# A gradient's forward D transform by even and odd d, with D in even/odd order in all tables

## The chip, the cores and the metric

The kernel runs on one core of one Trainium2 chip (trn2). The metric is the device time of one execution in microseconds. A profile's own span (first to last instruction) is some 1.8 us shorter than the time of the same execution. Ratios are the mean time of one kernel's runs over that of the other's runs of the same rounds on the same chip, with a 95% interval, so they are not quite the ratio of the medians that stand beside them. Times of the kernel before differ from chip to chip (medians of 1465.8 to 1468.0 us), so a kernel is compared with the kernel before of its own rounds.

## The reference

The forward function mixes a spectral filter and a gated feed-forward layer; the kernel returns its output and seven gradients.

```python
def _A_ref(x, w_r, w_i):                    # x: 1 x 2048 x 576
    X = rfft2(x.astype(float32), axes=(-2, -1)) * (w_r + 1j * w_i)
    return irfft2(X, s=(S, D), axes=(-2, -1)).astype(bfloat16)
def _B_ref(x, w_gate, w_up, w_down):        # D = 576, F = 4608
    return (_gelu(x @ w_gate) * (x @ w_up)) @ w_down
g = _sigmoid((x * gate_w).sum(-1, keepdims=True))
return g * a + (1 - g) * b                  # ... and its vjp for grad_out
```

The gradient with respect to the filter needs the forward transform of g * grad_out, as well as that of x. This is the transform that the change touches.

## The kernel before

The 2D transform is done by matmuls in steps. Step u1 takes one tile of 128 positions t (of 16), contracts D = 576 in five chunks with a table of cosines (c = 0) and sines (c = 1), and gives l = 0 to 288 (DF = 289) of each. Step u2 does the first part of the transform along S.

```python
def u1(t):
    def f():
        yps = ps()
        for c in range(2):
            for ci in range(5):
                nc.tensor.matmul(yps[:, c, :DF], lhsT=src[:, ci, t, :], rhs=tb.Dt[ci][:, c, :],
                                 start=(ci == 0), stop=(ci == 4))
        ys[t] = unit([2, DF], name="Y")
        # ... x: a plain copy; gradient:
        nc.scalar.activation(ys[t][:], yps[:, :, :DF], ACT.Copy, scale=scale[:, t:t + 1])
    return f
```

The gradient's units are not run by themselves. They are slots between the matmuls of the feed-forward part, which goes over 18 groups g of features, four iterations m in each: z and xy on PE, elementwise steps on DVE and ACT, and from g = 1 on the weight gradients of the group before, again on PE. In group 0 each iteration takes four slots; these are u1 of t = 0 to 8 and u2 of t = 0 to 6. The other seven u1 come later. After them come a middle part (filter products), then the inverse transforms, in the same slots.

Each group's weights are loaded one group ahead, in three parts after the first three iterations. The SP queue issues these loads and most stores of this stage, in order (POOL issues those of the weight gradients):

```python
if part < 2:
    w, cols = (B_w_gate, B_w_up)[part], slice(part * FG, (part + 1) * FG)
    LD.dma_start(wgu[:, 0:4, cols], w[0:512, fsl].rearrange("(c p) f -> p c f", p=P))
    for r in (LO, HI):
        LD.dma_start(wgu[r, 4, cols], w[512:D, fsl])
else:
    LD.dma_start_transpose(wdT[:, 4:5, :], B_w_down[fsl, DCH[4][0]:D])
    LD.dma_start_transpose(wdT[:, 0:4, :], B_w_down[fsl, 0:512])
    LD.dma_start(wdT[LO, 4, :], wdT[HI, 4, :])
```

In the middle part, ACT copies a result from PSUM to a tile Vt, which takes one of 19 rotating "unit" buffers, and SP stores it to DRAM (scr_p).

Of the kernel before, what the change touches and what calls it, by code (L numbers as in the profile page):

```python
# [9 lines left out]
ACT = mybir.ActivationFunctionType  # L10
ALU = mybir.AluOpType
BF16 = mybir.dt.bfloat16
# [27 lines left out]
LO, HI = slice(0, 64), slice(64, 128)  # L40
L2 = DF - P
L2NEW = 256 - L2


class Unit:
# [13 lines left out]
def iotas(nc, res, unit):  # L59
    tb = Tables()  # L60
    G = nc.gpsimd
    kw = dict(allow_small_or_imprecise_dtypes=True)
    tb.lrow = unit([DF], F32, name="lrow")
    G.iota(tb.lrow[:], pattern=[[1, DF]], base=0, channel_multiplier=0, **kw)
    tb.dcol = res.tile([P, 5], F32, name="dcol")
    G.iota(tb.dcol[:, 0:4], pattern=[[128, 4]], base=0, channel_multiplier=1, **kw)
    G.iota(tb.dcol[:, 4:5], pattern=[[0, 1]], base=512, channel_multiplier=1, **kw)
    tb.krow = res.tile([P, P], F32, name="krow")
    G.iota(tb.krow[:], pattern=[[1, P]], base=0, channel_multiplier=0, **kw)
    tb.scol = res.tile([P, T], F32, name="scol")  # L70
    G.iota(tb.scol[:], pattern=[[1, T]], base=0, channel_multiplier=16, **kw)
    tb.mrow_i = res.tile([P, P], I32, name="mrow_i")
    G.iota(tb.mrow_i[:], pattern=[[1, P]], base=0, channel_multiplier=0)
    tb.qcol_i = res.tile([P, 1], I32, name="qcol_i")
    G.iota(tb.qcol_i[:], pattern=[[0, 1]], base=0, channel_multiplier=1)
    tb.halfpi = res.tile([P, 1], F32, name="halfpi")
    nc.vector.memset(tb.halfpi[:], math.pi / 2)
    tb.pi = res.tile([P, 1], F32, name="pi")
    nc.vector.memset(tb.pi[:], math.pi * EPS_SCALE)
    tb.npi = res.tile([P, 1], F32, name="npi")  # L80
    nc.vector.memset(tb.npi[:], -math.pi * EPS_SCALE)
    tb.warm = res.tile([P, 1], F32, name="warm")
    nc.scalar.activation(tb.warm[:], tb.halfpi[:], ACT.Sin)
    tb.late = []
    return tb
# [7 lines left out]
def build_D(nc, tb, unit, res):  # L93

    V = nc.vector
    tb.Dt = []
    dn = res.tile([P, 5], F32, name="dn")
    V.tensor_scalar(dn[:], tb.dcol[:], 1.0 / D, None, op0=ALU.mult)
    step = 2.0 * math.pi / D
    for c0 in range(0, 5, 2):  # L100
        n = min(2, 5 - c0)
        TS = (nc.gpsimd if c0 == 4 else V).tensor_scalar
        X = unit([n, DF], F32, name="XD")
        y = unit([n, DF], F32, name="yD")
        for c in range(n):
            TS(y[:, c, :], tb.lrow[:], dn[:, c0 + c:c0 + c + 1], MAGIC, op0=ALU.mult, op1=ALU.add)
        TS(y[:], y[:], -MAGIC, -float(D), op0=ALU.add, op1=ALU.mult)
        for c in range(n):
            V.scalar_tensor_tensor(X[:, c, :], tb.lrow[:], tb.dcol[:, c0 + c:c0 + c + 1], y[:, c, :],
                                   op0=ALU.mult, op1=ALU.add)  # L110
        o = unit([n, 2, DF], name="Dt")
        V.scalar_tensor_tensor(y[:], X[:], -1.0, X[:], op0=ALU.mult, op1=ALU.max)

        r = LO if c0 == 4 else slice(0, P)
        if c0 == 4:
            nc.gpsimd.memset(o[HI, :, :, :], 0.0)

        def sines(o=o, X=X, y=y, r=r):
            nc.scalar.activation(o[r, :, 0, :], y[r], ACT.Sin, bias=tb.halfpi[r], scale=-step)
            nc.scalar.activation(o[r, :, 1, :], X[r], ACT.Sin, scale=-step * EPS_SCALE)  # L120
        tb.late.append(sines)
        tb.Dt += [o[:, c] for c in range(n)]


def build_R(nc, tb, unit, t0):
# [48 lines left out]
def kernel(  # L174
# [34 lines left out]
    dB = wstack.enter_context(tc.tile_pool(name="pdB", bufs=1)).tile([P, T, D], BF16, name="dB")  # L209

    wts = {}

    def load_w(g, part):

        fsl = slice(g * FG, (g + 1) * FG)
        if part == 0:
            wgu = wpool.tile([P, 5, 2 * FG], BF16, tag="wgu", name="wgu")
            wdT = wpool.tile([P, 5, FG], BF16, tag="wdT", name="wdT")
            wts[g] = wgu, wdT
        wgu, wdT = wts[g]  # L220
        if part < 2:
            w, cols = (B_w_gate, B_w_up)[part], slice(part * FG, (part + 1) * FG)
            LD.dma_start(wgu[:, 0:4, cols], w[0:512, fsl].rearrange("(c p) f -> p c f", p=P))
            for r in (LO, HI):
                LD.dma_start(wgu[r, 4, cols], w[512:D, fsl])
        else:
            LD.dma_start_transpose(wdT[:, 4:5, :], B_w_down[fsl, DCH[4][0]:D])
            LD.dma_start_transpose(wdT[:, 0:4, :], B_w_down[fsl, 0:512])
            LD.dma_start(wdT[LO, 4, :], wdT[HI, 4, :])

    nc.gpsimd.memset(gwT[LO, 4:5], 0.0)
    ident = res.tile([P, P], BF16, name="ident")
    make_identity(nc, ident[:])
    tb = iotas(nc, res, unit)
    with nc.allow_non_contiguous_dma(reason="tiny gate_w column load"):
        nc.gpsimd.dma_start(gwT[:, 0:4], gate_w[0:512].rearrange("(c p) -> p c", p=P))
        nc.gpsimd.dma_start(gwT[HI, 4:5], gate_w[512:D].rearrange("(p o) -> p o", o=1))

    def load_x(t0):
# [39 lines left out]
    def tchunk(src, dst, t0):  # L279
        for k, cs in enumerate(((0, 1), (2, 3), (4,))):  # L280
            pool, tag = headps()
            tp_ = pool.tile([P, 2, 2, 4, P], BF16, tag=tag, name="tp")
            for j, c in enumerate(cs):
                for tt in range(4):
                    if c < 4:
                        nc.tensor.transpose(tp_[:, 0, j, tt, :], src[:, t0 + tt, c * P:(c + 1) * P], ident[:])
                    else:
                        for r in (LO, HI):
                            nc.tensor.transpose(tp_[r, 0, 0, tt, :], src[:, t0 + tt, 512:D], ident[:])
            o = dst[:, cs[0]:cs[0] + len(cs), t0:t0 + 4, :]  # L290
            i = tp_[:, 0, 0:len(cs)]
            if k == (t0 // 4) % 2:
                nc.scalar.copy(o, i)
            else:
                V.tensor_copy(o, i)
# [189 lines left out]
    def fwd_units(src, dst, scale, ps=pftile, vevac=None):  # L485
# [16 lines left out]
        def u2(t):  # L502
# [12 lines left out]
                    nc.scalar.copy(Vt[:], vps[:, :, :DF])  # L515
                LD.dma_start(dst[t], Vt[:])
            return f
        return [u1(t) for t in range(T)], [u2(t) for t in range(T)]

    def tail_table():  # L520

        nc.gpsimd.memset(tb.At2[:], 0.0)
        LD.dma_start(tb.At2[L2NEW:P, :, :], tb.Dt[2][0:DF - 256, :, :])

    def zipped(u1, u2):
        out = [u1[0]]
# [129 lines left out]
    def inv_units(s, dv, scale):  # L656
        vp, zt = {}, {}

        def pre(i0):
            def f():  # L660
                vp[i0] = load_V(s, i0)
            f.noslot = True
            return f

        def z(i):
            def f():
                Vp = vp[i // 2 * 2]
                ii = i % 2
                zps = pftile()
                zf = zps[:].rearrange("p a b -> p (a b)")  # L670
                for lc, l0 in enumerate((0, P, L2)):
                    o = zf[:, lc * 256:(lc + 1) * 256]
                    for v in range(2):
                        nc.tensor.matmul(o, lhsT=Vp[:, ii, v, l0:l0 + P],  # L674
                                         rhs=tb.B[:, 1 - v:3 - v, :].rearrange("q v m -> q (v m)"), start=(v == 0), stop=(v == 1))
                zt[i] = unit([6, P], name="ZT")
                nc.scalar.copy(zt[i][:].rearrange("p a m -> p (a m)"), zf[:, 0:768])
            return f

        def d(i):  # L680
            def f():
                Z = zt.pop(i)
                yps = pftile()
                for c in range(2):
                    for lc in range(3):
                        nc.tensor.matmul(yps[:, c, :DF], lhsT=Z[:, 2 * lc + c, :],  # L686
                                         rhs=tb.Dt[lc][:, c, :] if lc < 2 else tb.At2[:, c, :],
                                         start=(lc == 0), stop=(lc == 2))
                ev = unit([2, DF], F32, name="ev")
                yo = unit([D], name="yo")  # L690
                nc.scalar.activation(ev[:], yps[:, :, :DF], ACT.Copy, scale=scale)
                V.tensor_tensor(yo[:, 0:DF], ev[:, 0, :], ev[:, 1, :], op=ALU.add)
                V.tensor_tensor(yo[:, D - 1:DF - 1:-1], ev[:, 0, 1:DF - 1], ev[:, 1, 1:DF - 1], op=ALU.subtract)
                LD.dma_start(dv[:, i, :], yo[:])
            return f
        out = [z(0)]
        for i in range(1, T):
            out += [z(i), d(i - 1)]
            if i % 2 == 1 and i + 3 < T:
                out.append(pre(i + 3))  # L700
        return out + [d(T - 1)], [pre(0), pre(2)]
# [23 lines left out]
    build_B(nc, tb, unit, res)  # L725
    run_late(tb)
    tail_table()
    x2[T - 1]()
    gate()

# [348 lines left out]
```

## Time and profile before

| | before |
|---|---|
| time, median of 6 (the result's rounds) | 1465.84 us (1463.18 to 1466.31) |
| profiled span | 1462.4 us |
| PE / DVE / ACT / POOL busy | 98% / 58% / 47% / 8% |
| u1 of the gradient | 160 matmuls of 289 columns, 124 ns apart |
| group 0, iteration | 10.25 us |
| bound in group 0 (65 to 105 us) | DVE |
| bound after that | PE |

The shares are averages over stages with different limits.

### The profile page before, as it was taken

How to read it: one execution, taken by the hardware profiler on the slowest of the kernel's cores; microseconds unless marked ns; L12 is line 12 of the kernel's file. 1: busy time of each engine (PE TensorE's matmuls, PEld its weight loads, DVE VectorE, ACT ScalarE, POOL GpSimd, SP SyncE). 2: the span in 40 equal slices, each digit the busy share in tenths (PEclk: the TensorE clock that was granted, in tenths of full speed). 3: DMA queues.
4: the chain of work that ended last, by engine and by line, in shares of the span. 5: the costliest groups of instructions: out<-in, count | busy, mean ns of one | idle time of the engine just before them, and what ended most of it. 6: DMA issues, size and time to landing. Idle time of an engine off the chain costs nothing.

```text
span 1462.4 us, 30015 instructions
## 1 busy us (share of the span) xinstructions
PE 1433.0 (98%) x11723; PEld 1068.6 (73%) x11808; DVE 846.0 (58%) x2258; ACT 690.7 (47%) x1355; POOL 118.3 (8%) x203
## 2 busy tenths in 40 slices
PE   7999999999999999999999999999999999999998
PEld 5766777677777677677677677678877777777776
DVE  7697677888887886776776776773000541211100
ACT  5786666766676666666766766662000000000000
POOL 1001011011011001001000000110000100000000
PEclk9999999999999999999999999999999999999999
DMA  5144344455445435334434544657999997878773
GB/s 190 60 127 123 114 126 120 140 146 150 137 132 148 120 117 142 106 110 134 136 104 119 147 126 113 168 135 169 260 195 197 211 205 160 171 157 166 154 149 72
DMA packets 483963, 210.49 MB, mean 144 GB/s; under 512 B 307883, under 2 KB 473932, under 8 KB 483820
## 3 DMA queue, kind: packets, MB, share of 16 engines
q1 hardware_dynamic: 474220, 188.06, 53.6%
q0 software_dynamic: 7792, 19.49, 4.4%
q8 instruction: 92, 1.51, 0.4%
q10 hardware_dynamic: 1808, 1.02, 0.3%
q14 instruction: 51, 0.42, 0.1%
HBM read 40.89 MB, written 93.82 MB: 92 GB/s over the span
## 4 chain that ended last, share of the span: by engine, by line
PE 92%; DVE 3%; issue 1%; ACT 1%; DMA 0%; DVEq 0%; ACTq 0%
PE acc L929 29%; PE wps L443 17%; PE xy L333 16%; PE wps L426 9%; PE z L321 8%; PE wps L456 2%; PE xy L328 2%; PE pf L686 2%; PE z L324 1%; PE pf L674 1%; PE pf L493 1%; PE fx L493 0%; DVE Vt L513 0%; DMA pin<-scr 0%; PE pf L632 0%
## 5 line engine op out<-in xcount | busy, mean ns | idle before, releaser
L929 PEld LDWEIGHTS <-pin 128*128 128x128 bf16 x3456 | 338.0, 98 | 87.1 <-DMA pin<-scr 1.9
L333 PE MATMUL xy<-wgu,xT 128*128 128x512 bf16 x1067 | 257.7, 380 | 9.6 <-issue 7.6
L443 PEld LDWEIGHTS <-xn 128*128 128x128 bf16 x2304 | 225.4, 98 | 32.4 <-issue 0.2
L333 PEld LDWEIGHTS <-xT 128*128 128x128 bf16 x1152 | 106.8, 98 | 137.3 <-issue 29.9
L346 ACT ACTIVATE da<-z,omg 128x256 bf16<-128x256 f32 x288 | 113.2, 474 | 148.0 <-PE z L324 145.0
L946 ACT COPY bo<-acc 128x288 f32<-128x288 f32 x32 | 12.7, 398 | 309.9 <-PE acc L929 251.8
L426 PE MATMUL wps<-dB,A 128*128 128x288 bf16 x1152 | 154.2, 286 | 0.0
L929 PE MATMUL acc<-wd_all,pin 128*128 128x288 bf16 x1152 | 142.8, 286 | 1.6 <-DMA pin<-scr 1.6
L929 PE MATMUL acc<-wgT,pin 128*128 128x288 bf16 x1152 | 143.6, 286 | 0.0
L929 PE MATMUL acc<-wuT,pin 128*128 128x288 bf16 x1152 | 143.6, 286 | 0.0
L321 PE MATMUL z<-wdT,dOT 128*128 128x256 bf16 x1152 | 137.7, 273 | 1.5 <-ACT Y L499 1.2
L426 PEld LDWEIGHTS <-A 128*128 128x128 bf16 x1152 | 112.7, 98 | 35.7
L443 PE MATMUL wps<-dHg,xn 128*128 128x256 bf16 x1152 | 134.4, 273 | 0.0
L443 PE MATMUL wps<-dHu,xn 128*128 128x256 bf16 x1152 | 131.5, 273 | 0.0
L321 PEld LDWEIGHTS <-dOT 128*128 128x128 bf16 x1152 | 111.2, 98 | 18.8 <-issue 5.6
L1003 DVE SCALAR_TENSOR_TENSOR f32t<-gwf,dlog,b16t 128x576 f32<-128x576 f32 x16 | 13.1, 818 | 187.5 <-DMA b16t<-dxa_scr 187.5
L352 ACT ACTIVATE q<-xy 128x512 bf16<-128x512 f32 x144 | 86.0, 597 | 69.6 <-PE xy L333 66.0
L359 DVE TENSOR_SCALAR s<-q 128x512 bf16<-128x512 bf16 x144 | 42.8, 297 | 94.2 <-ACT q L352 92.6
L376 ACT ACTIVATE om<-s 128x512 bf16<-128x512 bf16 x144 | 91.9, 638 | 8.9 <-DVE s L360 8.7
L377 ACT ACTIVATE s<-s 128x512 bf16<-128x512 bf16 x144 | 90.8, 630 | 4.6
L449 POOL DMA_DIRECT2D out_dram<-dw x67 | 48.7, 727 | 540.2 <-ACT dw L404 277.0
L360 DVE TENSOR_TENSOR s<-xb,s 128x512 bf16<-128x512 bf16 x144 | 61.3, 426 | 49.4 <-ACT xb L357 42.8
(182 smaller groups left out, 1807.3 us busy)
## 6 DMA issues: line engine op xcount, KB each, us to landing
scr<-A SPq DMA_DIRECT2D x144, 128.0 KB, 2.1
scr<-dHg SPq DMA_DIRECT2D x144, 128.0 KB, 2.1
scr<-dHu SPq DMA_DIRECT2D x144, 128.0 KB, 2.0
out_dram<-dw POOLq DMA_DIRECT2D x67, 128.0 KB, 2.6
wd_all<-in_B_w_down_dram SPq DMA_DIRECT2D x3, 1728.0 KB, 13.5
out_dram<-dwd POOLq DMA_DIRECT2D x34, 144.0 KB, 2.3
scr_p<-Vt SPq DMA_DIRECT2D x32, 144.5 KB, 2.2
Vp<-scr_p SPq DMA_DIRECT2D x16, 289.0 KB, 3.0
```

The source lines that it names most:

```text
L321: nc.tensor.matmul(zo(t), lhsT=dOT[:, ci, t, :], rhs=wdT[:, ci, :], start=(t % 4 < 2 and ci == 0), stop=False)
L333: nc.tensor.matmul(xy[k][:, t % 2, :], lhsT=xT[:, ci, t, :], rhs=wgu[:, ci, :], start=False, stop=(ci == 3))
L346: nc.scalar.activation(da[:, tt, :], z[:, tt, k, :], ACT.Copy, scale=omg32[:, t:t + 1])
L352: nc.scalar.activation(q[:], xy[:, :, 0:FG], ACT.Square)
L359: V.tensor_scalar(s[:], q[:], A_GELU, 1.0, op0=ALU.mult, op1=ALU.add)
L360: V.tensor_tensor(s[:], xb[:], s[:], op=ALU.mult)
L376: nc.scalar.activation(om[:], s[:], ACT.Sigmoid, scale=-2.0 * C_GELU)
L377: nc.scalar.activation(s[:], s[:], ACT.Sigmoid, scale=2.0 * C_GELU)
L426: nc.tensor.matmul(wps[:, :288], lhsT=tl(0, t)[:, fch * P:(fch + 1) * P], rhs=dB[:, t, h * 288:(h + 1) * 288], start=(t == 0), stop=(t == ...
L443: nc.tensor.matmul(wps[:, cc, :], lhsT=xn[:, t, (c0 + cc) * P:(c0 + cc + 1) * P], rhs=tl(k, t), start=(t == 0), stop=(t == T - 1))
L449: wst[0].dma_start(ov[:, c0:c0 + TPB, fsl], dw[:])
L929: nc.tensor.matmul(acc[:, :288], lhsT=src[:, r, :], rhs=w_of(r)[:, h * 288:(h + 1) * 288], start=(first and r == 0), stop=(last and r == F ...
```

## The change

With l and 288 - l, cosines and sines differ only in sign by the parity of d. So one sum over even d and one over odd d, for l = 0 to 144 only, give all 289 l: their sum is Y[l], their difference is Y[288 - l] reversed. That needs D on the partitions in even/odd order. Chunks 0 and 1 become the even d, 2 and 3 the odd ones; the last 64 d stay together and get a table masked by parity. Since all transforms share the tables, x, dOT and the weights are put into that order too.

```diff
+def half_units(u1):
+    def u(t):
+        def f():
+            yps = pftile()
+            for par in range(2):
+                for j, (ci, tab) in enumerate(((2 * par, tb.Dt[2 * par]), (2 * par + 1, tb.Dt[2 * par + 1]), (4, tb.half[:, par]))):
+                    nc.tensor.matmul(yps[:, par, :2 * HF].rearrange("p (c l) -> p c l", c=2), lhsT=dOT[:, ci, t, :],
+                                     rhs=tab[:, :, 0:HF], start=(j == 0), stop=(j == 2))
+            ev = unit([2, 2, HF], F32, name="ev")
+            Y = u1[t] = unit([2, DF], name="Y")
+            nc.scalar.activation(ev[:].rearrange("p e c l -> p e (c l)"), yps[:, :, :2 * HF], ACT.Copy, scale=g32[:, t:t + 1])
+            E = nc.gpsimd if t < 7 else V
+            E.tensor_tensor(Y[:, :, 0:HF], ev[:, 0], ev[:, 1], op=ALU.add)
+            for c in range(2):
+                E.tensor_tensor(Y[:, c, DF - 1:HF - 1:-1], ev[:, c, c, 0:HF - 1], ev[:, 1 - c, c, 0:HF - 1], op=ALU.subtract)
 ... (load_w)
-        if part < 2:  (w_gate in part 0, w_up in part 1)
+        if part == 0:  (both)
+            for w, c0 in ((B_w_gate, 0), (B_w_up, FG)):
+                cols = slice(c0, c0 + FG)
+                LD.dma_start(wgu[:, 0:4, cols].rearrange("p (e k) f -> p e k f", e=2),
+                             w[0:512, fsl].rearrange("(k p e) f -> p e k f", e=2, p=P))
+                for r in (LO, HI):
+                    LD.dma_start(wgu[r, 4, cols], w[512:D, fsl])
+        elif part == 1:  (the transposes of w_down, the large one into wtmp)
+        else:            (four copies wtmp -> wdT that sort the rows, and wdT[HI] -> wdT[LO])
 ... (build_D, tchunk, the inverse's z and d)
+            nc.tensor.transpose(tp_[:, 0, j, tt, :], src[:, t0 + tt, eo(c)], ident[:])
+                for lc, ls in enumerate((eo(0), eo(2), slice(L2, DF))):
```

More of the change, by code (lines that the diff above doesn't have):

```diff
@@ L42, with eo @@
 L2NEW = 256 - L2
+HF = 145
+def eo(c):
+    return slice(256 * (c % 2) + c // 2, 256 * (c % 2) + 256, 2)
 class Unit:
@@ L65, in iotas @@
     tb.dcol = res.tile([P, 5], F32, name="dcol")
-    G.iota(tb.dcol[:, 0:4], pattern=[[128, 4]], base=0, channel_multiplier=1, **kw)
+    for k in range(2):
+        G.iota(tb.dcol[:, 2 * k:2 * k + 2], pattern=[[1, 2]], base=256 * k, channel_multiplier=2, **kw)
     G.iota(tb.dcol[:, 4:5], pattern=[[0, 1]], base=512, channel_multiplier=1, **kw)
@@ L122, in build_D @@
         tb.Dt += [o[:, c] for c in range(n)]
+    tb.Dt[1], tb.Dt[2] = tb.Dt[2], tb.Dt[1]
 def build_R(nc, tb, unit, t0):
@@ L211 @@
     wts = {}
+    wtmp = [None]
     def load_w(g, part):
@@ L216, in load_w @@
         if part == 0:
-            wgu = wpool.tile([P, 5, 2 * FG], BF16, tag="wgu", name="wgu")
-            wdT = wpool.tile([P, 5, FG], BF16, tag="wdT", name="wdT")
-            wts[g] = wgu, wdT
-        wgu, wdT = wts[g]
-        if part < 2:
-            w, cols = (B_w_gate, B_w_up)[part], slice(part * FG, (part + 1) * FG)
-            LD.dma_start(wgu[:, 0:4, cols], w[0:512, fsl].rearrange("(c p) f -> p c f", p=P))
-            for r in (LO, HI):
-                LD.dma_start(wgu[r, 4, cols], w[512:D, fsl])
-        else:
-            LD.dma_start_transpose(wdT[:, 4:5, :], B_w_down[fsl, DCH[4][0]:D])
-            LD.dma_start_transpose(wdT[:, 0:4, :], B_w_down[fsl, 0:512])
+            wts[g] = (wpool.tile([P, 5, 2 * FG], BF16, tag="wgu", name="wgu"), wpool.tile([P, 5, FG], BF16, tag="wdT", name="wdT"))
+            wgu = wts[g][0]
+            for w, c0 in ((B_w_gate, 0), (B_w_up, FG)):
[4 more added lines that the diff above has]
+                    LD.dma_start(wgu[r, 4, cols], w[512:D, fsl])
+        elif part == 1:
+            wtmp[0] = wpool.tile([P, 4, FG], BF16, tag="wtmp", name="wtmp", bufs=1)
+            LD.dma_start_transpose(wts[g][1][:, 4:5, :], B_w_down[fsl, DCH[4][0]:D])
+            LD.dma_start_transpose(wtmp[0][:], B_w_down[fsl, 0:512])
+        else:
+            wdT = wts[g][1]
             LD.dma_start(wdT[LO, 4, :], wdT[HI, 4, :])
+            for par in range(2):
+                for h, r in enumerate((LO, HI)):
+                    LD.dma_start(wdT[r, 2 * par:2 * par + 2, :], wtmp[0][par:P:2, h:4:2, :])
     nc.gpsimd.memset(gwT[LO, 4:5], 0.0)
@@ L235 @@
     with nc.allow_non_contiguous_dma(reason="tiny gate_w column load"):
-        nc.gpsimd.dma_start(gwT[:, 0:4], gate_w[0:512].rearrange("(c p) -> p c", p=P))
+        for par in range(2):
+            nc.gpsimd.dma_start(gwT[:, 2 * par:2 * par + 2], gate_w[par:512:2].rearrange("(k p) -> p k", p=P))
         nc.gpsimd.dma_start(gwT[HI, 4:5], gate_w[512:D].rearrange("(p o) -> p o", o=1))
@@ L285, in tchunk @@
                     if c < 4:
-                        nc.tensor.transpose(tp_[:, 0, j, tt, :], src[:, t0 + tt, c * P:(c + 1) * P], ident[:])
+                        nc.tensor.transpose(tp_[:, 0, j, tt, :], src[:, t0 + tt, eo(c)], ident[:])
                     else:
@@ L517, in u2, with half_tails @@
             return f
-        return [u1(t) for t in range(T)], [u2(t) for t in range(T)]
+        return ([u1(t) for t in range(T)] if src is xT else half_units(ys)), [u2(t) for t in range(T)]
     def tail_table():
         nc.gpsimd.memset(tb.At2[:], 0.0)
-        LD.dma_start(tb.At2[L2NEW:P, :, :], tb.Dt[2][0:DF - 256, :, :])
+        for par in range(2):
+            LD.dma_start(tb.At2[L2NEW + par:P:2], tb.Dt[1 + 2 * par][0:17 - par])
+    def half_tails():
+        mi = res.tile([P, 1], I32, name="par_i")
+        V.tensor_single_scalar(mi[:], tb.qcol_i[:], 1, op=ALU.bitwise_and)
+        mask = res.tile([P, 2], F32, name="par_f")
+        V.tensor_copy(mask[:, 1:2], mi[:])
+        V.tensor_scalar(mask[:, 0:1], mask[:, 1:2], -1.0, 1.0, op0=ALU.mult, op1=ALU.add)
+        tb.half = unit([2, 2, HF], name="half")
+        for par in range(2):
+            V.tensor_scalar(tb.half[:, par], tb.Dt[4][:, :, 0:HF], mask[:, par:par + 1], None, op0=ALU.mult)
+    def half_units(u1):
+        def u(t):
+            def f():
+                yps = pftile()
+                for par in range(2):
+                    for j, (ci, tab) in enumerate(((2 * par, tb.Dt[2 * par]), (2 * par + 1, tb.Dt[2 * par + 1]), (4, tb.half[:, par]))):
[8 more added lines that the diff above has]
+                    E.tensor_tensor(Y[:, c, DF - 1:HF - 1:-1], ev[:, c, c, 0:HF - 1], ev[:, 1 - c, c, 0:HF - 1], op=ALU.subtract)
+            return f
+        return [u(t) for t in range(T)]
     def zipped(u1, u2):
@@ L670, in f @@
                 zf = zps[:].rearrange("p a b -> p (a b)")
-                for lc, l0 in enumerate((0, P, L2)):
+                for lc, ls in enumerate((eo(0), eo(2), slice(L2, DF))):
                     o = zf[:, lc * 256:(lc + 1) * 256]
                     for v in range(2):
-                        nc.tensor.matmul(o, lhsT=Vp[:, ii, v, l0:l0 + P],
+                        nc.tensor.matmul(o, lhsT=Vp[:, ii, v, ls],
                                          rhs=tb.B[:, 1 - v:3 - v, :].rearrange("q v m -> q (v m)"), start=(v == 0), stop=(v == 1))
@@ L686, in f @@
                         nc.tensor.matmul(yps[:, c, :DF], lhsT=Z[:, 2 * lc + c, :],
-                                         rhs=tb.Dt[lc][:, c, :] if lc < 2 else tb.At2[:, c, :],
+                                         rhs=tb.Dt[2 * lc][:, c, :] if lc < 2 else tb.At2[:, c, :],
                                          start=(lc == 0), stop=(lc == 2))
@@ L727 @@
     tail_table()
+    half_tails()
     x2[T - 1]()
```

## The prediction

> **What bounds the kernel now.** I read the page first (busy shares, slices, costly groups), then the busy time by stretch, then the chain of work that ended last for the stretch in which the gradient's forward transform starts, and last the timeline there.
>
> ```profile
> PE 1433.0 (98%) x11723; PEld 1068.6 (73%) x11808; DVE 846.0 (58%) x2258; ACT 690.7 (47%) x1355; POOL 118.3 (8%) x203
> L493 PE MATMUL pf<-Dt,dOT 128*128 128x289 bf16 x160 | 22.2, 287 | 1.1 <-DVE Vt L513 1.0
> ```
>
> PE is busy nearly everywhere, and the changed matmuls are the 160 of line 493 on dOT. The mean of 287 ns is the trap here: matmuls overlap, so it is a latency and not what one costs. The cost is the spacing. The chain shows it:
>
> ```profile
> 57.95 2.48 PE pf L493 x20
> 60.42 1.73 PE xy L333 x8
> 62.65 1.25 PE pf L493 x10
> 63.98 0.74 ACT Y L499
> 64.72 0.53 ACT om L376
> 65.27 0.43 DVE om L381
> ...
> 102.21 2.24 DVE dB L774 x8
> 104.45 0.68 DVE Vt L513
> 105.17 1.40 PE pf L493 x10
> 106.57 1.75 PE wps L443 x16
> ```
>
> Twenty matmuls of 289 columns take 2.48 us, so 124 ns each. The second thing to see is more important: from 65.27 to 105.17 us the chain is on DVE (so are all the pieces that I left out at the "..."). Before and after it is on PE. That stretch is the first feature group (g = 0), which has no weight gradients to give PE work. The stretches say the same (columns: window, then busy time of PE, PEld, DVE, ACT, POOL):
>
> ```profile
> 75.02:85.28 10.26, 9.86 (x68) 6.08 (x69) 9.71 (x27) 8.55 (x17) 0.00 (x0) 1.00 0.48 138
> 300.00:600.00 300.00, 297.08 (x2375) 214.51 (x2403) 245.75 (x654) 202.99 (x404) 29.45 (x46) 1.00 0.48 136
> ```
>
> In the first of them, one of the group's four iterations (10.26 us), DVE works 9.71 us with no named wait. PE's 9.86 is inflated by the overlap: by spacing I count 16 z matmuls 1.75, 16 full xy 3.6, half-depth ones 0.7, two D transforms 2.5, two S transforms 1.0, in all about 9.5 us. From 300 to 600 us it is PE that is full and DVE has 18% to spare.
>
> [...]
>
> **Part 1, fewer matmuls.** Per t, 10 matmuls of 289 columns become 6 of 290: 10 x 124 - 6 x 124.5 = 493 ns less PE time. Sixteen units give 7.9 us (0.54%), the ceiling of the change; with the latency of 287 ns it would have looked like 18 us. Where do they lie? Group 0 takes four transform slots in each of four iterations, 16 slots, which are u1 of t = 0 to 8 and u2 of 0 to 6. So nine units lie in group 0 and seven in the PE-bound rest. **Seven units: -3.45 us on the path.** Of the nine, t = 0 and 1 (the x20 piece) lie before DVE takes over; ACT evicts Y twice there and only then copies xb, on which DVE waits:
>
> ```profile
> 61.71 0.43 DVE L360 TENSOR_TENSOR s<-xb,s 128x512 bf16<-128x512 bf16 x1 [2.80 <-ACT xb L357]
> ```
>
> PE is 0.99 us earlier there. But the new half tables put five small DVE operations (three of about 0.16 us by the rows for one column, two of about 0.2 us) in front of omg, for which ACT waits 0.72 us, so ACT is some 0.5 us later and then continuous: omg, four da, q, two Y, xb. I count xb to start at 60.35 instead of 61.10: **-0.75 us**. The other seven of group 0 shorten PE beside a busy DVE: **0**.
>
> **Part 2, the combination.** Y was one ACT eviction (742 ns). Now the eviction goes to f32 (580 columns; the inverse's ev shows that f32 output is no slower) and three additions follow, of 290, 144 and 144 elements, on POOL for t < 7 and on DVE from 7 on. On DVE the like operation is this one:
>
> ```profile
> 700.47 0.47 DVE L692 TENSOR_TENSOR yo<-ev 128x289 bf16<-128x289 f32 x1 [1.66 <-ACT ev L691]
> 700.84 0.45 DVE L693 TENSOR_TENSOR yo<-ev 128x287 bf16<-128x287 f32 x1
> 701.21 0.29 DVE L359 TENSOR_SCALAR s<-q 128x512 bf16<-128x512 bf16 x1
> ```
>
> It costs 0.37 us of spacing; 144 elements about 0.22; so 0.81 us for one Y. For t = 7 and 8, inside DVE's stretch: **+1.6 us**. From t = 9 on it falls on a DVE with slack: 0.
>
> [...] But POOL is not free for DVE. The start of the program shows it:
>
> ```profile
> 3.61 1.20 DVE L109 SCALAR_TENSOR_TENSOR XD<-lrow,dcol,yD 128x289 f32<-128x289 f32 x2
> 7.22 0.95 DVE L109 SCALAR_TENSOR_TENSOR XD<-lrow,dcol,yD 128x289 f32<-128x289 f32 x2
> ```
> ```profile
> 3.90 0.60 POOL L106 TENSOR_SCALAR yD<-lrow,dn 128x289 f32<-128x289 f32 x1
> ```
>
> The same DVE pair takes 0.25 us longer beside one POOL operation of 0.60 us. Line 112 is 0.11 us longer beside POOL's 0.52 us. Together DVE lost a third of POOL's time (0.36 of 1.12). [...] I choose 0.5 per Y, because the author's boundary at t < 7 hints that POOL was found cheaper than DVE's 0.81. Y of t = 0 meets an idle DVE; t = 1 to 6 meet a full one: 6 x 0.5 = **+3.0 us**.
>
> **Part 3, order and tables.** Group weights: 13 transfers instead of 9 per group, one contiguous transpose into a temporary and 256 KB copied inside SBUF; they are issued an iteration or more before use, with DMA under half busy: 0. Strided loads (128 transposes in the head, 128 of Vp in the inverse): 0. Startup: one more iota and gate_w transfer on POOL, about 0.1 us on dn: 0. The store queue starts some 2 us later behind four more copies, with units to spare: 0.
>
> **Sum:** -3.45 - 0.75 + 1.6 + 3.0 = +0.4 us, so 1465.9 us.
>
> **The rivals.** [...] (b) POOL is free for DVE, or DVE's stretch gives way to the shorter PE: ACT waits 0.87 us per iteration for line 493 before Y. Then 1465.55 - 3.45 - 0.75 + 1.6 = 1463, and 1458 if all 7.9 us come through. Against: the chain does not touch PE there. (c) Weight loads with a step of two are slow. If they took 196 ns instead of 98, the 128 loads of Vp would space their matmuls by 196 instead of 109 ns: +11 us, in the inverse's stretch. (d) Y arrives late for u2: between u1 and u2 of an odd t lie only 3.4 us[...]. A late u2 would delay z on PE, which has 0.7 us slack per iteration; at worst +1 us per pair, some +3.
>
> **Range and chances.** [...] the gain is capped at 7.9 us. I take 1460 to 1473. Over 2% would need 29 us either way: faster is impossible by part 1 (0.01), slower would need a surprise in strided loads or in the weights' transfers (0.02).
>
> **What would show each step.** Line 493's twin on dOT: 96 matmuls of 290 columns, spaced 124 ns. [...] DVE in group 0: operations beside POOL lengthened by 0.1 to 0.4 us, iterations of 10.7 to 11.3 us instead of 10.25; the chain on DVE until about 108 to 109 instead of 105.17. After that PE shorter by 3.45 us. Line 674's weight loads at 98 ns. The prediction is wrong if iterations of group 0 become shorter (b), [...] or if time is lost after 590 us, where the inverse begins (c).

The passages that no trace or run of this case showed are cut from it: a paragraph that rested on none, the estimate of how long POOL's additions take, rival (a), which was built on it, and the clauses that use it. The four terms of the sum stand, and it came to +0.4 us, 1465.9 us. But behind the +3.0 only the author's choice of 0.5 us per Y is left, and the range of 1460 to 1473 was chosen with a cut term in view as well. Two more of its figures are estimates of the author that the trace of the kernel before did not show: 0.22 us for 144 elements (beside 0.37 us measured for 289), and 0 for the strided loads. That f32 output is no slower on ACT is measured there: 652 ns for ev of the inverse (f32) and 652 for Xg (bf16), both a copy of 578 columns with a constant scale.

## The result

The changed kernel takes 1467.78 us in the median (six runs, 1466.13 to 1471.53) against 1465.84 us of the kernel before. The ratio is 1.0019, interval 1.0005 to 1.0033: the change is slower by about 0.2%, within 2%. The page's busy line of the changed kernel (busy us and share of each engine, instructions):

```profile
PE 1425.1 (97%) x11659; PEld 1061.7 (72%) x11744; DVE 857.0 (58%) x2290; ACT 690.0 (47%) x1355; POOL 131.6 (9%) x226
```

PE has less to do, DVE and POOL more, and the time is not shorter. Groups of instructions of the changed kernel (count, then busy us and mean ns): 64 and 32 matmuls instead of 160 (their means are latencies again), POOL's large addition at 0.77 us, and the strided weight loads of the inverse, whose mean is still 98 ns:

```profile
L559 PE MATMUL pf<-Dt,dOT 128*128 128x290 bf16 x64 | 12.5, 286 | 3.9 <-ACT da L361 2.9 <-DVE Vt L528 1.0
L559 PE MATMUL pf<-half,dOT 128*128 128x290 bf16 x32 | 9.1, 285 | 0.0
L565 POOL TENSOR_TENSOR Y<-ev 128x290 bf16<-128x290 f32 x7 | 5.4, 771 | 67.1 <-ACT ev L563 67.1
L720 PEld LDWEIGHTS <-Vp 128*128 128x128 bf16 x192 | 18.8, 98 | 5.8
```

**Group 0.** The chain that ended last, at the end of the first stretch:

```profile
105.09 2.24 DVE dB L821 x8
107.33 0.68 DVE Vt L528
108.05 0.91 PE pf L559 x6
108.95 1.75 PE wps L458 x16
```

DVE hands over to PE at 108.05 us instead of 105.17. One iteration (columns as in the prediction: window, busy us of PE, PEld, DVE, ACT, POOL) is 11.19 us long instead of 10.26, with DVE at 10.63 instead of 9.71:

```profile
76.31:87.50 11.19, 8.90 (x62) 5.14 (x62) 10.63 (x26) 8.53 (x16) 3.44 (x6) 1.00 0.51 140
```

The timeline shows how DVE loses that. In the kernel before, two of its elementwise operations in such an iteration take 0.43 and 0.29 us; in the changed kernel the same two stand beside POOL's additions and take 0.73 and 0.53 us (before, then after; lines of other engines are left out):

```profile
74.50 0.43 DVE L360 TENSOR_TENSOR s<-xb,s 128x512 bf16<-128x512 bf16 x1
74.84 0.29 DVE L361 TENSOR_SCALAR q<-q 128x512 bf16<-128x512 bf16 x1
```
```profile
73.95 0.71 POOL L565 TENSOR_TENSOR Y<-ev 128x290 bf16<-128x290 f32 x1 [1.66 <-ACT ev L563]
74.21 0.73 DVE L375 TENSOR_TENSOR s<-xb,s 128x512 bf16<-128x512 bf16 x1
74.62 1.07 POOL L567 TENSOR_TENSOR Y<-ev 128x144 bf16<-128x144 f32 x2
74.87 0.53 DVE L376 TENSOR_SCALAR q<-q 128x512 bf16<-128x512 bf16 x1
```

**Where the two executions part.** The clearest view is the start of the four half-depth z matmuls, once per iteration, 72 times in each trace. The difference to the kernel before, in us (negative is earlier), for the main kernels of this document:

| iteration (start in before) | changed | changed, 2nd run | e_full | e_nocomb | e_dve | e_late | e_late_split |
|---|---|---|---|---|---|---|---|
| g 0, m 0 (54.96) | -0.84 | -0.84 | -0.83 | -0.83 | -0.83 | -0.84 | +0.01 |
| g 1, m 0 (97.37) | +0.73 | +0.67 | -0.83 | -2.43 | +2.27 | -0.98 | -0.14 |
| g 1, m 1 (111.97) | +2.38 | +2.35 | -0.83 | -2.60 | +3.83 | -1.48 | -0.64 |
| g 2, m 2 (178.92) | -0.31 | -0.34 | -0.84 | -5.57 | +1.13 | -4.18 | -3.33 |
| g 4, m 3 (295.01) | +4.14 | +4.10 | +2.24 | -2.38 | +5.80 | +0.71 | -1.39 |
| g 17, m 3 (989.45) | +4.14 | +4.10 | +2.24 | -2.38 | +5.81 | +0.72 | -1.38 |
| end of the span | +3.1 | +6.4 | +3.8 | +1.9 | +6.9 | +1.8 | -1.1 |

Three things are to be seen in the column of the changed kernel. Until 112 us it falls behind (group 0). From there to 179 us it wins back 2.7 us, the shorter transforms on PE, and is 0.31 us ahead. Then, near 282 us, it loses 4.45 us in one place, and never again until the last group. That last loss is in no term of the prediction. The last row adds what differs in the final stage, where all programs are the same: the wait for the first tiles of that stage and the clock there change the distance to the kernel before by -1.0 to +4.3 us in these runs.

**The place near 282 us.** Waits of the changed kernel from 265 to 290 us (who waited for what: us in total, times, longest):

```profile
ACT Vt L683 <- DMA scr_p<-Vt: 3.0, 1, 3.0
PE z L336 <- ACT Vt L683: 2.7, 1, 2.7
```

ACT's copy into Vt waits until the store of an earlier Vt has landed; PE's z needs the PSUM tile that this copy frees. That the copy waits because it reuses the earlier Vt's buffer is read from the source, and no run tested it. PE then pays a second time: in the two windows that follow, its granted clock (the column after POOL) is 0.96 and 0.62 instead of 1.00.

```profile
280.00:284.00 4.00, 1.31 (x11) 1.05 (x10) 3.86 (x11) 0.64 (x1) 0.00 (x0) 0.96 0.26 89
284.00:288.00 4.00, 3.78 (x20) 1.74 (x20) 2.27 (x6) 1.57 (x4) 0.71 (x1) 0.62 0.59 146
```

The z matmuls after the wait take 2.79 us instead of 1.75 (before, then after, from the chains of work):

```profile
280.38 1.75 PE z L321 x16
```
```profile
282.79 2.79 PE z L336 x16
```

The missing clock is 0.04 x 4 + 0.38 x 4 = 1.7 us of full rate, and with the wait of 2.7 us it makes up the 4.45 us. This second payment is not sure to come. It also followed the wait in after_again, e_dve, e_late, e_actq and e_late_tf (waits of 2.6 to 3.1 us; with the changed kernel six runs, in which 1.7 to 2.1 us were lost besides the wait), but not in e_full, e_nocomb, e_res and e_lump (2.5 to 3.0 us), whose steps are 0.1 to 0.2 us more than their waits. So the steps of two runs can differ by 1.7 us without any difference in the store. Why was the store late? SP's queue in the kernel before, then in the changed kernel:

```profile
273.27 0.46 SPq L223 DMA_DIRECT2D wgu<-in_B_w_gate_dram  x1
...
275.07 0.53 SPq L612 DMA_DIRECT2D out_dram<-o  x1
...
276.21 4.08 SPq L638 DMA_DIRECT2D scr_p<-Vt  x3
```
```profile
272.70 0.64 SPq L230 DMA_DIRECT2D wgu<-in_B_w_gate_dram  x1
...
274.72 0.65 SPq L230 DMA_DIRECT2D wgu<-in_B_w_up_dram  x1
...
278.29 4.79 SPq L684 DMA_DIRECT2D scr_p<-Vt  x3
```

The change moved w_up into part 0. Six weight transfers instead of three now stand ahead of the stores, and the first store of Vt is issued at 278.29 instead of 276.21 us, 2.08 us later. It takes 3.73 us to land, and ACT, which had been ready 3.0 us before, waited for it. In the kernel before nobody waits, but there is hardly any room: the first store lands 2.99 us after its issue, at 279.20, and ACT comes to the third Vt at 279.30 (before, then after):

```profile
279.30 0.64 ACT L637 CAST Vt<-pf 128x578 bf16<-128x578 f32 x1
```
```profile
282.10 0.64 ACT L683 CAST Vt<-pf 128x578 bf16<-128x578 f32 x1 [2.98 <-DMA scr_p<-Vt]
```

### The profile page after: what moved, and what is told of

The parts are those of the page before. It is cut to its first block, busy times and chain, and to the rows that moved or that the text cites. A ratio compares the mean times of both kernels' runs of the same rounds, so it can differ in the third digit from the quotient of the medians.

```text
span 1465.5 us, 30040 instructions
## 1 busy us (share of the span) xinstructions
PE 1425.1 (97%) x11659; PEld 1061.7 (72%) x11744; DVE 857.0 (58%) x2290; ACT 690.0 (47%) x1355; POOL 131.6 (9%) x226
## 4 chain that ended last, share of the span: by engine, by line
PE 91%; DVE 5%; ACT 1%; issue 1%; DMA 1%; POOL 0%; DVEq 0%; SPq 0%; ACTq 0%; POOLq 0%
PE acc L976 29%; PE wps L458 17%; PE xy L348 15%; PE wps L441 9%; PE z L336 8%; PE wps L471 2%; PE xy L343 2%; PE pf L732 2%; PE z L339 1%; PE pf L720 1%; PE fx L508 1%; DVE Vt L528 0%; DVE s L375 0%; PE tp L301 0%; DVE A L399 0%
```

## The experiments

Eleven runs were made, on three chips; one of them is the changed kernel again. Each is compared with the kernel before in its own rounds.

### e_full, e_split, e_res, e_late: whose is the loss near 282 us, and is group 0 bound by DVE?

**e_full**: the order of D stays, the half transform goes.

```diff
-        return ([u1(t) for t in range(T)] if src is xT else half_units(ys)), [u2(t) ...]
+        return [u1(t) for t in range(T)], [u2(t) ...]
-    half_tails()
```

> The even/odd order of D, its loads and its tables stay as in the changed kernel, but the gradient's forward D transform is the full one again (10 matmuls of 289 columns, one ACT eviction, no half table). Theory: the order itself costs PE and DVE nothing, so the iterations of group 0 are 10.25 us again. For the jump of 4.4 us near 282 us two rivals: (A) the weights' transfers, now issued in one lump ahead of the stores, delay the stores of Vt: then the jump is still there and the time is 1469 to 1471; (B) the half table keeps one of the 19 unit buffers: then there is no jump and the time is 1465 to 1466.5.

1469.19 us against 1466.73; ratio 1.0014 (1.0001 to 1.0026). In the table the column is flat: -0.83 at the start of group 0, -0.84 at 179 us. So the even/odd order, its strided loads and its extra copies cost PE and DVE nothing in all of that. Then comes the jump, 3.07 us in the same place. The half table isn't there, so rival (B) falls.

**e_split**: the changed kernel with w_gate in part 0, w_up and the transposes in part 1, the copies in part 2.

```diff
+        if part < 2:
             wgu = wts[g][0]
-            for w, c0 in ((B_w_gate, 0), (B_w_up, FG)):
+            for w, c0 in (((B_w_gate, 0), (B_w_up, FG))[part],):
 ...
-        elif part == 1:
+        if part == 1:
 ...
-        else:
+        if part == 2:
```

> The changed kernel with the weights' loads spread again: w_gate in part 0, w_up with the transposes in part 1, the copies in part 2. (A) the lump causes the jump near 282 us: it is gone, the time falls by about 4 us against the changed kernel, to 1463 to 1464.5. (B) the missing unit buffer causes it: it stays, 1467 to 1468.5.

1469.20 us, ratio 1.0017 (1.0004 to 1.0029). The trace says what (A) expects in part: PE waits 0.8 us for Vt instead of 2.7, and the step near 282 us is 1.0 us instead of 4.45. But the time did not fall: this execution lost 3.1 us more than the kernel before in the final stage (from +1.26 in the last group to +4.4 at the end), and the times of all five runs are no better. By time alone this run is inconclusive; e_late_split below repeats the remedy.

**e_res**: the half table in a buffer of its own (`hres.tile` instead of `unit`), so that 19 unit buffers rotate as before.

> The changed kernel with the half table in a buffer of its own, so that the 19 unit buffers are as free as before. (B): the jump near 282 us is gone, 1463 to 1464.5. (A): it stays, 1467 to 1468.5.

1469.58 us, ratio 1.0023 (1.0009 to 1.0036). The step near 282 us is still there (2.7 us, with a wait of ACT of 2.8 us for the same store and no loss of clock after it). (B) falls a second time.

**e_late**: the half transform only where PE is the bound.

```diff
-        return ([u1(t) for t in range(T)] if src is xT else half_units(ys)), ...
+        return ([u1(t) for t in range(T)] if src is xT else [u1(t) for t in range(9)] + half_units(ys)[9:]), ...
-                E = nc.gpsimd if t < 7 else V
+                E = V
+        if t == 12:              # in the loop over x's tiles in the head, instead of after it
+            half_tails()
```

> The half transform only from t = 9 on, where PE is the bound; t = 0 to 8, in the stretch that DVE bounds, are full again, all combinations that are left run on DVE, and the half table is built earlier in the head. Theory: iterations of group 0 back to 10.25 us, the chain on DVE until about 105 us, then PE shorter by 7 x 0.49 = 3.4 us. Against the kernel before: -3 us without the jump near 282 us (1462 to 1463.5), +1 us if the jump is still there (1466 to 1468). Rival, PE bounds group 0 too: then the half transform given up for nine units costs 4.4 us and the time is above that of the changed kernel.

1465.42 us against 1466.73; ratio 0.9992 (0.998 to 1.0005): the same as the kernel before. The iterations of group 0 are 10.25 us again (-0.97, -0.97, -0.98 at their starts). From group 1 to 179 us PE gains 3.20 us with the seven units. Then the jump costs 4.9 us. The rival, that PE bounds group 0 too, would have made it slower than the changed kernel.

### e_nocomb and e_dve: what a Y costs DVE, on POOL and on DVE itself

**e_nocomb** is wrong (the gradients of the filter weights have an error above 1): six matmuls, but Y is one ACT copy of the first 578 columns.

```diff
-                nc.scalar.activation(ev[:]..., yps[:, :, :2 * HF], ACT.Copy, scale=g32[:, t:t + 1])
-                E.tensor_tensor(...)   # all three
+                nc.scalar.activation(Y[:], yps[:, :, :DF], ACT.Copy, scale=g32[:, t:t + 1])
```

> Wrong result on purpose: the changed kernel with 6 matmuls per t, but without the three combinations; Y is one ACT eviction of the first 578 columns. Theory (group 0 is bound by DVE): its iterations take 10.2 to 10.3 us as before although PE has 1 us less to do in each, and the seven later units shorten PE by 3 to 3.4 us; the jump near 282 us stays. Rival (PE or ACT's wait for PE bounds group 0): iterations of 9.3 to 9.8 us.

1468.70 us against 1468.01; ratio 1.0006 (0.9989 to 1.0023). Its iteration (window, busy us of PE, PEld, DVE, ACT, POOL):

```profile
74.58:84.79 10.21, 9.02 (x61) 5.28 (x61) 9.66 (x26) 8.46 (x17) 0.00 (x0) 1.00 0.62 167
```

PE has a microsecond less to do in it than in the kernel before, and it is 10.21 us long instead of 10.25; the one before it is 9.97. In the three iterations from the second on PE's 3 us bring 0.43 us (-2.00 to -2.43). So DVE bounds the stretch: e_dve below, with more work on DVE, lengthens it by as much. Before DVE takes over, in the first iteration, the two shorter transforms bring 1.17 us, and from 97 to 179 us the later seven bring 3.14. At 179 us this kernel is 5.26 us ahead of the changed one: that is the price of the combinations, and it is more than the 4.7 us that the matmuls alone bring. The time does not show the 5 us for two reasons that the trace names: the jump (3.2 us) and 4.3 us more than the kernel before in the final stage of this execution.

**e_dve**: all combinations on DVE (`E = V`).

> The changed kernel with all combinations on DVE, none on POOL. Theory: a Y costs DVE 0.8 us instead of the 0.47 us that POOL's operations take from it, so an iteration of group 0 with two Y takes 11.8 to 11.9 us instead of 11.18, and the stretch ends 2 us later. [...]

1474.94 us, ratio 1.0046 (1.0024 to 1.0067).

```profile
76.96:88.80 11.84, 9.03 (x62) 5.28 (x62) 11.29 (x33) 8.58 (x16) 0.00 (x0) 1.00 0.47 128
```

An iteration with two Y takes 11.84 us, so a Y costs (11.84 - 10.21) / 2 = 0.81 us on DVE and (11.19 - 10.21) / 2 = 0.49 us of DVE's stretch when POOL does it. POOL's three operations for a Y take 0.77 + 2 x 0.51 = 1.8 us, of which DVE loses 27%, not all.

### e_lump and e_actq: is it the lump of weight transfers?

**e_lump** is the kernel before with one edit: w_up is loaded in part 0, after w_gate.

```diff
-        if part < 2:
-            w, cols = (B_w_gate, B_w_up)[part], slice(part * FG, (part + 1) * FG)
+        if part == 0:
+            for k, w in enumerate((B_w_gate, B_w_up)):
+                cols = slice(k * FG, (k + 1) * FG)
 ...
-        else:
+        elif part == 2:
```

> The kernel before with one edit: w_up is loaded in part 0 together with w_gate, as in the change. (A) the lump of six transfers ahead of the stores makes the jump: PE loses 2 to 4.5 us near 282 us at a wait of ACT's Vt for a store of Vt, and all else is as before, 1468 to 1470. If it does not show, the lump alone is not the cause, and something else of the change must be.

1471.42 us against 1468.01; ratio 1.0022 (1.0007 to 1.0037). All is as in the kernel before (-0.43 at every start up to group 4), then the step: +2.64 us in the same place and +0.98 at the start of group 5. The wait at the step:

```profile
ACT Vt L638 <- DMA scr_p<-Vt: 2.7, 1, 2.7
```

So the lump alone, without any of the transform's change, brings the same wait. This is the cleanest of the runs on (A).

**e_actq**: the changed kernel with the 32 stores of Vt in the middle part issued by ACT's queue (`nc.scalar.dma_start`).

> The changed kernel with the 32 stores of Vt in the middle part issued from ACT's queue, right behind the copy that makes Vt, instead of from SP's queue behind the weights. If the jump near 282 us is these stores waiting in SP's queue, it is gone: the position at 300 us is 0 to 0.5 us before that of the kernel before, and the time falls by about 4 us against the changed kernel, to 1463 to 1465. If it stays, the queue is not what delays them.

1476.21 us, ratio 1.0059 (1.0044 to 1.0074). It failed: the step near 282 us is 5.1 us, and two microseconds more are lost in three small steps later. The trace says why:

```profile
281.10 0.34 ACTq L684 DMA_DIRECT2D scr_p<-Vt  x1
281.49 0.63 ACT L391 ACTIVATE om<-s 128x512 bf16<-128x512 bf16 x1 [3.33 <-DMA wgu<-in_B_w_up_dram]
```

ACT had made this Vt by 278.16, but its issue was let go only at 281.10, and what the profile names as the releaser is the landing of w_up. The trace's semaphore numbers show how. The transfers of the SP and ACT queues tell of their landing on eight semaphores in rotation: 968 of 986 issues of the kernel before and 1041 of 1059 of the changed kernel use the number of the eighth issue before them. In 911 of 994 and 998 of 1067 the issue, or the instruction just before it, waits for that number, and no issue starts before the eighth transfer before it has landed (0 of the 862 and 927 for which the landing is recorded). This store's semaphore had been used by the third transfer of w_up, issued at 276.13; that one landed at 281.02, and ACT's wait for this semaphore ended at 281.06.

So the place in SP's queue was not the whole of (A). The stores are behind the weights in the rotation of semaphores too, whichever queue issues them, and ACT, which does other work, now stood still for it.

### e_late_split, e_late_tf, after_again: both remedies

**e_late_split** is e_late with e_split's order of loads.

> Both remedies together: the half transform only from t = 9 on (group 0 as before), and the weights' loads spread again as in e_split. Theory: -0.5 to -0.8 from a quicker head, -3.4 from seven shorter transforms, and near 282 us a loss of 0 to 1 us (e_split) instead of 4.5 (e_late): against the kernel before -3 us, a ratio of 0.998; the z matmuls of the last group start 3 to 4 us earlier than before. If the spread loads do not help here, it stays at e_late's 0.9992 and the jump is 3 us or more.

1462.79 us against 1467.08; ratio 0.9971 (0.9959 to 0.9983), and no run of it (1461.88 to 1463.06) reaches the fastest of the kernel before (1464.01). This version beats both kernels. In the trace group 0 is as before, 3.2 us are won from 97 to 179 us, and the step near 282 us is 1.9 us instead of e_late's 4.9:

```profile
ACT Vt L685 <- DMA scr_p<-Vt: 2.1, 1, 2.1
```

**e_late_tf** has the two transposes first, then w_gate, then w_up with the copies.

> As e_late_split with the parts in another order: the two transposes first (part 0), then w_gate, then w_up with the copies, so that only two transfers stand in front of the stores of the middle part at the place where the jump was. Theory (an issue waits for the eighth transfer before it): no jump at 282 us, 4 us ahead of the kernel before in the last group, ratio 0.997 to 0.998. Risk: the eight transfers of part 2 collide with other stores and make a jump elsewhere.

1465.59 us, ratio 0.9993 (0.9981 to 1.0005). My expectation was wrong: with only two transfers ahead of the stores the step is back, at 4.8 us (PE waits 3.0 us for Vt). The first store of Vt is issued at 273.94, but that is not early: PE is 4.12 us ahead of the kernel before here, so the store comes at 278.06 of that kernel's time, 1.85 us later than its 276.21. And it takes 4.56 us to land instead of 2.99. Besides, the copies of wdT come later in this order: z of group 1 waits 0.5 us for one, and the start there is -0.24 instead of e_late's -0.98.

The same reckoning for the other runs, in us. From each issue the run's distance to the kernel before at the start of g 4, m 1 is taken off, so that issues are compared at the same place of PE's work:

| | issue later than in before | landing longer than 2.99 | sum | ACT waited |
|---|---|---|---|---|
| changed | 2.39 | 0.74 | 3.13 | 2.98 |
| e_lump | 1.97 | 0.92 | 2.89 | 2.75 |
| e_late | 2.98 | 0.55 | 3.53 | 3.37 |
| e_late_tf | 1.85 | 1.57 | 3.42 | 3.27 |
| e_late_split | 1.45 | 0.74 | 2.19 | 2.05 |
| e_split | 0.00 | 1.25 | 1.25 | 1.11 |

The sum is the wait plus the 0.1 us of room that the kernel before has. In the first three runs, which have the lump, two thirds to five sixths of the sum are the later issue. In e_late_tf the later issue is not the number of transfers alone: 1.08 us of it were lost before the first weight transfer, where one issue of dHu's store took 1.75 us (0.37 in the kernel before); e_late_split has the same (1.85 us).

**after_again**: the changed kernel once more in these rounds.

> The changed kernel once more, on the same chip and in the same rounds as the two remedies. The jump near 282 us comes again (3 to 4.5 us), since it depends on the order of the transfers and not on chance; iterations of group 0 of 11.18 us; time 1.001 to 1.003 of the kernel before.

1471.49 us, ratio 1.0034 (1.0021 to 1.0046). The columns of the two runs of the changed kernel agree within 0.06 us in every row but the last: the step near 282 us is no accident. On these rounds e_late_split's median is 8.7 us under it.

## Why the prediction was right, point by point

The prediction said 1465.9 us, within 2%; measured were 1467.78, inside the range of 1460 to 1473. Its mechanism held, its sum was nearly right up to 179 us, and one term that it set to zero was not zero. Without the head's 0.84 us (below) the changed kernel stands at +0.53 us there, and the sum said +0.4. That the time came so near as well is partly luck: the step of 4.45 us is in no term, and in this trace the head gives 0.84 us of it back and the final stage 1.0.

- **Cost by spacing and not by latency.** Right. The 96 matmuls of 290 columns start 124 ns apart inside a transform, as the 160 of 289 did. From group 1 on the distance to the kernel before shrinks by 0.49 us with each shorter transform. Seven units were put at 3.45 us; e_late shows 3.20. The changed kernel shows 2.7 from g 1, m 1 on, with one of the seven already behind it; the last unit brings 0.23 us alone, where e_nocomb, without combinations, has 0.50.
- **Nine of sixteen units beside a busy DVE bring nothing.** Right for the seven beside the busy DVE, by e_nocomb: 0.43 us in three iterations where PE had 3 us less.
- **The start, -0.75.** Measured -0.63 in the changed kernel (-0.84 to -1.47), -1.17 without the combinations. The five operations for the half table were there and took 1.04 us (53.84 to 54.88), and ACT waited 1.41 us for omg instead of 0.72.
- **POOL, 0.5 us of DVE's time per Y.** Right: 0.49, but with luck. The trace of the kernel before has no such addition on POOL, so its length was not shown; 0.5 was picked because of the boundary at t < 7. That DVE loses a part and not all of POOL's time is what the start showed (0.36 of 1.12 us), and e_dve confirms that POOL is cheaper than DVE. POOL's operations take 0.77 and 0.51 us, where the same ones on DVE in the changed kernel take 0.457 and 0.303 (1.69 times). Of their 1.8 us per Y, DVE, which is busy for 10.63 of 11.19 us, loses 0.49, a little less than the third of the start. How much of POOL's recorded time was itself a wait no run shows.
- **DVE, 0.8 us per Y.** Right: 0.81. Together, 3.0 + 1.6 us were predicted and 5.26 measured between e_nocomb and the changed kernel, which includes the early part and small waits.
- **Strided loads.** Right, though the 0 was an estimate without a strided load in the trace: 98 ns for Vp's in the inverse and 98 ns in the head's transposes, as unstrided ones in the kernel before, and no start moves from 310 us to the last group, so rival (c) falls. Rival (d) did not show either: from 58 to 108 us no wait of PE for POOL's Y is named.
- **The end of DVE's stretch.** "About 108 to 109": 108.05, iterations "10.7 to 11.3": 11.19.
- **Part 3, group weights: 0.** This is the step that failed. It argued that the transfers come an iteration or more before they are used, with DMA under half busy. That looked at the weights' own readers. Of the stores behind them it looked only at the store queue's start ("with units to spare: 0"), not at the stores of Vt in the middle part, where the kernel before has 0.1 us to spare. The change put six loads ahead of them, and PE lost 4.45 us, of which 2.7 is the wait and the rest the reduced clock after it. The same edit alone gives a step of 2.6 us in the kernel before (e_lump).
- **A quicker head.** Not predicted: 0.84 us, and not the change's work. In the trace 0.71 us of it arises between two groups of PE work that start at 14.87 and 17.30 us in the kernel before, at 14.86 and 16.59 us in the changed one. The four matmuls of a transform that begins there are 240 ns apart in the kernel before (14.87, 15.11, 15.35, 15.59) and 120 to 130 ns in the changed one (14.86, 14.98, 15.11, 15.23): PE ran at half the rate for longer. The traces' records of the full clock begin at 16.3 us in the kernel before and 16.4 in e_late_split, which has no gain; at 15.4 and 15.5 in e_lump and e_res, which have 0.43 and 0.44 us; and at 13.3 to 14.5 in the nine others, which have 0.78 to 0.84. So the gain goes with the moment at which the full clock comes. Why it comes when it does stays open.

What stays open besides: why some stores take up to 1.6 us longer to land, why single issues of the SP queue take 1.3 to 1.9 us instead of 0.4 (in the kernel before too, once), and whether the stores of Vt, issued ahead of the weights or given more buffers, would remove the 1 to 2 us that remain with the spread loads.

## What to carry to other kernels

Ask for each unit of removed work which engine ends the stretch that it lies in: here the same edit is worth 0.49 us per unit in one stretch and costs up to 0.8 in the other, and the best version (0.9971) makes it only where it pays and spreads the loads. Work moved from a busy DVE to POOL is not free for DVE, but may be cheaper than on DVE itself (0.49 against 0.81 us). Moving loads about in a queue is a change of its own: look at which stores stand behind them, what waits for those stores to land, and how much time it has to spare. And before two traces are compared by position, look at the clock of both.
